# Windowed attention with a feed-forward layer on Trainium2: the order of the first loads, the split of the last stores, and a new table for the planner

## The chip, the core and the metric

The kernel runs on one core of one Trainium2 chip. A core has a matrix engine (TensorE, PE in the profile; its weight loads are PEld), VectorE (DVE), ScalarE (ACT), GpSimd (POOL) and SyncE (SP), each with its own instruction stream executed in order, and 16 DMA engines. SP and ACT issue the transfers here. The metric is the device time of one execution in microseconds.

## The reference

Eight batches of eight heads, 512 local and 32 global positions each, head size 64. Global queries attend to everything; local queries attend to the 32 global keys and to a window of 32 positions to either side. Then comes a feed-forward layer with a gate h - tanh(h).

```python
k_all = np.concatenate([k_g, k_l], axis=2)
v_all = np.concatenate([v_g, v_l], axis=2)
out_g = np.matmul(sm(scale * np.matmul(q_g, k_all.transpose(0, 1, 3, 2))), v_all)
s_ll = np.where(np.abs(pos[:, None] - pos[None, :]) <= 32, scale * np.matmul(q_l, k_l.transpose(0, 1, 3, 2)), -1e9)
s_lg = scale * np.matmul(q_l, k_g.transpose(0, 1, 3, 2))
out_l = np.matmul(sm(np.concatenate([s_lg, s_ll], axis=-1)), v_all)
x = np.concatenate([out_g, out_l], axis=2).transpose(0, 2, 1, 3).reshape(8 * 544, 512)
h = x @ w_in            # 512 -> 2048
return (h - np.tanh(h)) @ w_out
```

Here sm subtracts the row's maximum, takes the exponential and divides by the sum plus 1e-9.

## The kernel before

**Work and its parts.** The feed-forward layer runs in nine chunks: one of 512 local rows for each batch, and a last one, "g", with the 256 global rows of all batches. A chunk of local rows has 16 steps; each step has 12 matmuls into the hidden layer (L1136, or L1162 for the first steps of batch 0), then tanh on ACT (L1144), the subtraction on DVE (L1147), a rounding to the high part (L324, called through `copy`), the low part on POOL (L1153), and 12 matmuls into the output (L1199). Products that need precision are made of high and low parts in three passes.

The attention of the first two batches works on pairs of heads (class `Pair`): `add_load` brings keys and queries (L476), `add_turn` transposes them on PE (L493) and copies them into `first_kw` and `first_q`, `glob` copies the transposed global keys from `first_g` behind the windows of `first_kw`, `add_scores` makes the global queries' scores (L526, L527), their peaks on DVE (L532), exponentials on ACT (L537) and scaling on POOL (L545), turned on PE at L566; `add_local_scores` makes the local scores (L617), whose peaks are L884 (DVE), exponentials L891 (ACT), and scaling L904 (POOL), turned at L972. `add_products` multiplies with the values (L649). `add_first_globals` loads the global keys and queries of the first two batches (L435), one load for all eight heads, into `wraw3`. The later batches work head by head (class `Head`: L827, L828 for the global scores, L879, L880 for the local ones, L1053 and L1055 for products and turns), between the feed-forward matmuls of the batch before.

**Weights.** `add_weights` loads one of 32 tiles of 512 KB (L377), alternating between `wraw01` and a part of `first_q`; ACT rescales one half of each number (L388), DVE shifts the other (L392) and joins both (L397), the high part is rounded on ACT or DVE (L324), and POOL makes the low part (L403).

**Order.** Nothing is issued while it is written down: each step is given to `add` with its possible engines and costs, a due time, what it reads and writes, and its PSUM banks. `Order.run` then places the steps one by one: the one that can start earliest by the planner's own estimate, by due time among near equals, on the engine that suits. Due times and the penalties for one engine or the other come from the numbers in `CFG`. The dictionary `at` holds for each engine the time at which it is free, 0 at the start. What comes out is a fixed order for each engine.

**Transfers.** Nearly all are issued by SP. The first pair's keys and queries, four transfers, are issued by ACT; the global keys and queries and the first weights by SP. A chunk's output leaves through `out_copy` (a copy from PSUM to one of two buffers) and `out_dma`. For a local chunk the 128 rows of a tile lie together (L1229). For "g" a tile holds the 32 global rows of four batches, which lie 544 rows apart; L1231 writes them with one pattern of three dimensions:

```python
nc.sync.dma_start(bass.AP(out.tensor, out.offset + row * DM, [[step * DM, P // n], [DM, n], [1, DM]]), y)
```

Of the kernel before, what the change touches and what calls it, by code (L numbers as in the profile page):

```python
# [16 lines left out]
P = 128  # L17
# [32 lines left out]
class Order:  # L50
# [58 lines left out]
    def run(self):  # L109

        ready = [o for o in self.ops if o.n == 0]
        at = {}
# [5 lines left out]
        out = []  # L118
# [70 lines left out]
def kernel(ctx, tc, q_l, k_l, v_l, q_g, k_g, v_g, w_in, w_out, out):  # L189
    nc = tc.nc  # L190
# [3 lines left out]
    T = S + G  # L194
# [95 lines left out]
    def bank(shape, j, dt=F32):  # L290
# [6 lines left out]
        elif len(shape) == 4:  # L297
# [4 lines left out]
    CFG = dict(a_g=0.4467, a_gl=9.0702, a_kg=1.2994, a_kq=0.6435, a_ph=0.7195, a_qs=7.4639, a_v=2.7931, a_w=0.8782, a_wn=28.167, a_xg=24.0892,  # L302
               d_g=11.4807, d_gl=27.1005, d_kg=17.5448, d_kq=3.2824, d_ph=0.1724, d_pl=7.5682, d_qh=1.3047, d_qs=1.7431, d_tg=2.0404, d_tp=1.2696,
               d_v=43.1581, d_w=59.5639, d_wl=2.6144, d_wn=1.778, d_xg=14.9271, d_y=10.5287, gfirst=0, ho=12.4704, hs=5.8719, lag=14.1617, last=0.0,
               newb=2, o_ld=361.9221, o_pv=-2.1295, o_pvp=4.3749, o_s=-375.3617, o_sg=-28.1789, o_sp=31.7504, o_t=648.945, o_tg=45.2913,
               o_tn=-1106.6547, o_tpp=-433.7579, o_v=-410.0484, o_vr=-254.8525, one=0, p0=6.2738, pen=67.5481, penp=-32.1307, s_g=12.8404,
               s_gl=3.2481, s_kq=0.2136, s_p=46.7709, s_ql=1.9011, s_tg=1.375, s_v=8.7545, s_w=16.9623, s_wl=44.2573, step=15.8445, step1=4.7468,
               lag0=-307.9083, hs0=19.1353, tol=0.005, wd0=-185.6377, wsp=14.5594, xw=1.446, o_ld0=600.5133, o_tn0=224.9458, o_sg0=-83.4892,
               o_tg0=-104.0145, o_s0=-179.3281, o_sp0=-1012.5551, o_t0=617.9054, o_tpp0=232.7574, o_vl0=-205.8728, o_vl1=-1041.2318, o_pv0=816.5364,
               o_pvp0=61.9839, o_ld1=626.5193, o_pv1=-181.2357, o_pvp1=102.4522, o_s1=-119.6345, o_sg1=-827.2517, o_sp1=751.489, o_t1=311.7714,  # L310
               o_tg1=153.1303, o_tn1=-150.4646, o_tpp1=837.4523, o_v1=-236.5332, o_vr1=258.8109, wsp1=4.8097, ho0=596.7105, mw=0.0485, o_h0=507.8294,
               hp=-176.4382, bp0=180.6731, bp1=36.9715, bp2=87.4305, bp3=49.379, kd=0.0002)
# [115 lines left out]
    def add_first_globals(b):  # L428
# [4 lines left out]
        def load(a):  # L433
            def fn(e, _):
                nc.sync.dma_start(raw[a].rearrange("s (h d) -> s h d", h=H), (k_g, q_g)[a][b].rearrange("h s d -> s h d"))  # L435
            return fn
# [1020 lines left out]
```

## Time and profile before

| | |
|---|---|
| median of 3 runs (lowest to highest) | 1022.02 us (1020.94 to 1023.49) |
| the profiled execution's own time | 1022.42 us |
| its span, first to last instruction | 1020.6 us |
| PE busy | 991.1 us, 97% |
| DVE, ACT, POOL busy | 617.7, 653.3, 615.2 us |
| DMA moved | 91.67 MB, 90 GB/s on average |
| granted TensorE clock, mean | 0.997 |

The profile shows one execution. Busy times are of an engine's instructions alone; the times at which it waits, and who ended the wait, stand in a view of their own. Rows of the timeline give start and length in us, engine, line, operation, tiles written and read, how many were merged, and in brackets the idle time before and its releaser. "SPq" and "ACTq" are the sequencers that issue transfers: the length is that of the issue, not of the transfer.

### The profile page before, as it was taken

The numbers are of one execution on the slowest core, as the hardware profiler recorded it, in microseconds if no ns is written. First come the engines' busy times: TensorE is split into PE (matmuls) and PEld (weight loads), VectorE is DVE, ScalarE is ACT, GpSimd is POOL, SyncE is SP. The second block draws the span as 40 slices with busy tenths as digits, with TensorE's granted clock in tenths as the row PEclk, the third lists the DMA queues.
The fourth block names the chain that finished last, engine by engine and source line by source line (L and its number), as shares of the span: only waits on it lengthen the run. The fifth ranks groups of instructions, "written<-read, shape, count | busy, mean of one in ns | idle before, by whom it ended". The sixth has DMA issues, their size and how long they took to land.

```text
span 1020.6 us, 18634 instructions
## 1 busy us (share of the span) xinstructions
PE 991.1 (97%) x5648; PEld 825.3 (81%) x5648; DVE 617.7 (61%) x1877; ACT 653.3 (64%) x1732; POOL 615.2 (60%) x839
## 2 busy tenths in 40 slices
PE   6999999999999999999999999999999999999996
PEld 4777777887878888888888888888887888888895
DVE  6975665687758764777658774777657774221010
ACT  5867656776768765877568775887668774322221
POOL 4665656676767765677657775677657774322221
PEclk9999999999999999999999999999999999999998
DMA  8564644543354333543354432543255330100000
GB/s 212 142 161 142 175 125 101 131 88 81 70 124 103 83 84 68 132 89 83 64 116 110 89 84 57 143 88 84 57 109 122 83 74 10 42 1 1 31 11 22
DMA packets 250701, 91.67 MB, mean 90 GB/s; under 512 B 204520, under 2 KB 238056, under 8 KB 250600
## 3 DMA queue, kind: packets, MB, share of 16 engines
q1 hardware_dynamic: 248488, 89.95, 37.8%
q8 instruction: 45, 0.74, 0.3%
q10 hardware_dynamic: 2112, 0.52, 0.2%
q14 instruction: 56, 0.46, 0.1%
HBM read 49.27 MB, written 8.91 MB: 57 GB/s over the span
## 4 chain that ended last, share of the span: by engine, by line
PE 83%; ACT 5%; DVE 3%; issue 2%; DMA 2%; SPq 2%; POOL 2%; ACTq 0%; DVEq 0%; POOLq 0%
PE bank L1199 33%; PE bank L1136 30%; PE bank L1053 5%; PE bank L1055 4%; PE bank L879 2%; PE bank L880 2%; PE bank L649 1%; PE bank L972 1%; ACT prob L891 1%; PE bank L617 1%; PE bank L526 1%; PE bank L1162 1%; SPq L687 1%; DMA first_raw<-in_q_l_dram 1%; PE bank L493 1%
## 5 line engine op out<-in xcount | busy, mean ns | idle before, releaser
L1199 PE MATMUL bank<-w_out_hi,gates 128*128 128x512 f32 x1088 | 302.2, 396 | 0.7 <-ACT wraw L324 0.3
L1153 POOL TENSOR_TENSOR gates<-t,gates 128x512 fp32r<-128x512 f32 x136 | 175.4, 1290 | 177.9 <-PE bank L1199 128.0
L1199 PEld LDWEIGHTS bank<-w_out_hi,gates 128*128 128x128 f32 x1088 | 198.5, 188 | 42.9 <-POOL gates L1153 2.3
L1147 DVE TENSOR_TENSOR t<-bank,t 128x512 f32<-128x512 f32 x136 | 94.0, 692 | 170.8 <-ACT t L1144 169.5
L1144 ACT ACTIVATE t<-bank 128x512 f32<-128x512 f32 x136 | 81.3, 598 | 133.8 <-PE bank L1136 124.7
L1199 PE MATMUL bank<-w_out_lo,gates 128*128 128x512 f32 x544 | 152.3, 394 | 0.0
L1136 PE MATMUL bank<-x_hi,w_in_hi 128*128 128x512 f32 x496 | 137.5, 399 | 0.0
L1136 PE MATMUL bank<-x_hi,w_in_lo 128*128 128x512 f32 x496 | 133.7, 391 | 0.0
L1136 PE MATMUL bank<-x_lo,w_in_hi 128*128 128x512 f32 x496 | 133.5, 391 | 0.0
L904 POOL TENSOR_SCALAR prob<-prob,stats 128x224 f32<-128x224 f32 x240 | 107.8, 463 | 40.4 <-DVE stats L628 13.9
L324 ACT CAST gates<-t 128x512 fp32r<-128x512 f32 x136 | 84.3, 621 | 59.7 <-PE bank L1199 41.1
L891 ACT ACTIVATE prob<-prob,stats 128x224 f32<-128x224 f32 x240 | 113.7, 475 | 11.2 <-DVE stats L884 10.4
L1199 PEld LDWEIGHTS bank<-w_out_lo,gates 128*128 128x128 f32 x544 | 100.6, 188 | 20.1
L884 DVE CUSTOM_DVE_ANT_0 prob<-bank,mask 128x224 f32<-128x224 f32 x240 | 81.6, 388 | 51.6 <-PE bank L880 39.4
L1136 PEld LDWEIGHTS bank<-x_lo,w_in_hi 128*128 128x128 f32 x496 | 91.3, 188 | 18.4
L1136 PEld LDWEIGHTS bank<-x_hi,w_in_lo 128*128 128x128 f32 x496 | 90.9, 188 | 17.9
L324 ACT COPY wraw<-bank 64x288 f32<-64x288 f32 (+1 forms) x130 | 58.0, 446 | 69.2 <-PE bank L1053 45.3
L1136 PEld LDWEIGHTS bank<-x_hi,w_in_hi 128*128 128x128 f32 x496 | 87.8, 189 | 14.9 <-issue 0.4
L1055 PE MATMUL bank<-idr,prob 128*128 128x128 f32 x376 | 98.0, 280 | 0.4 <-DVE stats L839 0.2
L1053 PE MATMUL bank<-thi,vv 128*128 128x160 f32 (+2 forms) x384 | 96.8, 294 | 1.6 <-DVE stats L839 0.8
L1053 PE MATMUL bank<-tlo,vv 128*64 128x160 f32 (+2 forms) x384 | 89.3, 234 | 0.3 <-POOL tlo L951 0.3
L1088 POOL TENSOR_TENSOR x_lo<-wraw,x_hi 64x256 fp32r<-64x256 f32 x96 | 70.4, 734 | 29.3 <-DVE x_hi L324 20.9
(144 smaller groups left out, 1780.8 us busy)
## 6 DMA issues: line engine op xcount, KB each, us to landing
hl<-hl SPq DMA_DIRECT2D x72, 128.0 KB, 2.3
out_dram<-wraw SPq DMA_DIRECT2D x34, 256.0 KB, 2.4
kw<-hl SPq DMA_DIRECT2D x72, 96.0 KB, 2.2
wraw<-in_moe_w_in_dram SPq DMA_DIRECT2D x12, 512.0 KB, 4.7
rawkq<-in_k_l_dram SPq DMA_DIRECT2D x96, 64.0 KB, 2.3
rawkq<-in_q_l_dram SPq DMA_DIRECT2D x96, 64.0 KB, 2.3
vraw<-in_v_l_dram SPq DMA_DIRECT2D x48, 128.0 KB, 2.4
kw<-hl SPq DMA_DIRECT2D x72, 80.0 KB, 2.1
```

The source lines that it names most:

```text
L324: (nc.scalar.copy if e == "A" else nc.vector.tensor_copy)(dst, src)
L884: nc.vector.tensor_tensor_reduce(out=self.tile(t)[:, :KC], in0=getattr(self, f"s_{pair}")[:, i, :KC], in1=tile_mask[t], scale=-0.125, scal ...
L891: nc.scalar.activation(x, x, AF.Exp, bias=self.st[:, t:t + 1], scale=-1.0, accum_out=self.st[:, 4 + t:5 + t])
L904: nc.gpsimd.tensor_scalar(x, x, self.st[:, 8 + t:9 + t], 1.0, op0=ALU.mult, op1=ALU.mult)
L1053: nc.tensor.matmul(dst, l, r, start=i == 0, stop=i == len(mm) - 1, skip_group_check=True)
L1055: nc.tensor.transpose(*turns[i // each], idn)
L1088: eng[e].tensor_sub(places()[1], view(total, [(160, 2), (1, P)]), f32(places()[0]))
L1136: nc.tensor.matmul(self.h[s][:, j * n:(j + 1) * n], w[:, cc, f * P:(f + 1) * P], self.x()[xi][:, cc, :n], start=part == 0 and cc == 0 and ...
L1144: nc.scalar.activation(tt_[q], self.h[s], AF.Tanh)
L1147: nc.vector.tensor_sub(tt_[q], self.h.pop(s), tt_[q])
L1153: eng[e].tensor_sub(gg[q][1], tt_[q].rearrange("p (k c) -> p k c", k=4), f32(gg[q][0]))
L1199: nc.tensor.matmul(self.acc[tt], g[:, j * nt + tt], low_out(f) if wi else w_out_hi[:, f], start=s == 0 and k == 1, stop=last and k == 3 * ...
```

## The change

Four edits in the code, and a new table:

1. The first pair's keys stay on ACT's queue, its queries move to SP's queue; both come first, through due times of -1002 and -1001.
2. The global keys and queries of batch 0 move from SP to ACT, behind the first pair's keys (due time -1000).
3. For "g", each tile is written with four transfers of 32 rows in place of one: two from SP, two from ACT.
4. The planner takes every engine (T, A, D, P, S: PE, ACT, DVE, POOL, SP) to be free from 0.7 on, not from 0.
5. All numbers of `CFG` that set due times and penalties are new.

```diff
-        at = {}
+        at = dict.fromkeys("TADPS", 0.7)
...
-    CFG = dict(a_g=0.4467, a_gl=9.0702, a_kg=1.2994, a_kq=0.6435, a_ph=0.7195, a_qs=7.4639, a_v=2.7931, a_w=0.8782, a_wn=28.167, a_xg=24.0892,
+    CFG = dict(a_g=0.3833, a_gl=1.5118, a_kg=1.3108, a_kq=0.24, a_ph=0.0029, a_qs=9.8856, a_v=2.7859, a_w=0.9693, a_wn=28.6019, a_xg=24.9592,
...
-                nc.sync.dma_start(raw[a].rearrange("s (h d) -> s h d", h=H), (k_g, q_g)[a][b].rearrange("h s d -> s h d"))
+                eng[e].dma_start(raw[a].rearrange("s (h d) -> s h d", h=H), (k_g, q_g)[a][b].rearrange("h s d -> s h d"))
...
-            add(("S", 0.6), load(a), due - 100, w=[keys[a]], xfer=0.36)
+            add(("S" if b else "A", 0.6), load(a), due - 100 if b else -1000, w=[keys[a]], xfer=0.36)
...
-                add(("S" if self.j else "A", 1.1), load(a, (k_l, q_l)[a]), self.due(self.C["o_ld"] - 8) if self.j else -200 + a,
+                add(("S" if self.j or a else "A", 1.1), load(a, (k_l, q_l)[a]), self.due(self.C["o_ld"] - 8) if self.j else -1002 + a,
...
-                    def out_dma(e, _, tt=tt, key=key):
-                        y = wraw[key[1]]
-                        row, n, step = self.dst(tt)
-                        if n == P:
-                            nc.sync.dma_start(out[row:row + P, :], y)
-                        else:
-                            nc.sync.dma_start(bass.AP(out.tensor, out.offset + row * DM, [[step * DM, P // n], [DM, n], [1, DM]]), y)
+                    def out_dma(part):
+                        def fn(e, _, tt=tt, key=key):
+                            y = wraw[key[1]]
+                            for row, lo, hi in part:
+                                eng[e].dma_start(out[row:row + hi - lo, :], y[lo:hi])
+                        return fn
...
-                    add(("S", 0.6), out_dma, due + 0.5, r=[key], w=[("out", self.name, tt)], xfer=0.73)
+                    runs = self.dst(tt)
+                    k = max(1, len(runs) // 2)
+                    add(("S", 0.6 * k), out_dma(runs[:k]), due + 0.5, r=[key], w=[("out", self.name, tt)], xfer=0.73)
+                    if runs[k:]:
+                        add(("A", 0.6 * k), out_dma(runs[k:]), due + 0.5, r=[key], w=[("out", self.name, tt, 1)], xfer=0.73)
...
     def local_rows(b):
-        return lambda i: (b * T + G + i * P, P, 0)
+        return lambda i: [(b * T + G + i * P, 0, P)]
 
     def global_rows(i):
-        return i * (P // G) * T, G, T
+        return [((i * (P // G) + j) * T, j * G, (j + 1) * G) for j in range(P // G)]
```

What stands where now, at the places that the prediction speaks of. First SP's queue at the start of the program, with - for the rows of before and + for those of the changed kernel (`first_raw` and `rawkq` take keys and queries of a pair, `first_v` its values, `wraw_70` the global keys and queries, `wraw_65` and the weight load's `first_q` are the two buffers for raw weights):

```order
+L476 DMA first_raw<-in_q_l_dram 128x4x64 x2
+L588 DMA first_v<-in_v_l_dram 128x7x64
+L588 DMA first_v<-in_v_l_dram 96x64
+L588 DMA first_v<-in_v_l_dram 64x8x64
+L600 DMA first_v<-in_v_g_dram 32x4x64 x2
+L377 DMA wraw_65<-in_moe_w_in_dram 128x4x256
+L377 DMA first_q<-in_moe_w_in_dram 128x4x256
+L476 DMA first_raw<-in_k_l_dram 128x4x64 x2
+L476 DMA first_raw<-in_q_l_dram 128x4x64 x2
+L476 DMA rawkq<-in_k_l_dram 128x4x64 x2
+L476 DMA rawkq<-in_q_l_dram 128x4x64 x2
 L435 DMA wraw_70<-in_k_g_dram 32x8x64
```

Before, SP began with the two loads of L435 (batch 0's, now on ACT), then the two weight tiles, then the values; now it has the first pair's queries, then the values, then the two weight tiles. ACT at the same place, behind the program's first branch:

```order
 L476 DMA first_raw<-in_k_l_dram 128x4x64 x2
-L476 DMA first_raw<-in_q_l_dram 128x4x64 x2
+L435 DMA wraw_70<-in_k_g_dram 32x8x64
+L435 DMA wraw_70<-in_q_g_dram 32x8x64
 L324 ACT_TABLE_LOAD
-L324 COPY first_g<-bank_96 128x128
-L324 COPY first_m<-bank_96 64x4x32 x2
+L324 COPY first_g<-bank_97 128x128
+L324 COPY first_m<-bank_97 64x4x32 x2
 L388 ACTIVATE wraw_65<-wraw_65 128x512
 L324 COPY first_kw<-first_g 128x4x32 x2
```

The queries have left, the global loads have come; the broadcast of the global keys (`first_kw<-first_g`) stands behind the first weight step (L388) in both. DVE's first work on data, before:

```order
L324 COPY first_kw<-bank_95 128x2x160
L392 TENSOR_SCALAR wraw_65<-wraw_65 128x512
L397 SCALAR_TENSOR_TENSOR vraw<-wraw_65 128x512
L324 COPY first_q<-bank_97 128x512
L392 TENSOR_SCALAR first_q<-first_q 128x512
L532 ISA pg,stats<-bank_98,first_m 64x512
L532 ISA stats 64x1
L532 ISA pg,stats<-bank_99,first_m,stats 64x96
L532 ISA stats 64x1
L397 SCALAR_TENSOR_TENSOR wraw_66<-first_q 128x512
L884 ISA prob_92,stats<-bank_100,mask_89 128x224
```

and in the changed kernel:

```order
L324 COPY first_kw<-bank_95 128x2x160
L324 COPY first_q<-bank_96 128x512
L392 TENSOR_SCALAR wraw_65<-wraw_65 128x512
L397 SCALAR_TENSOR_TENSOR vraw<-wraw_65 128x512
L392 TENSOR_SCALAR first_q<-first_q 128x512
L397 SCALAR_TENSOR_TENSOR wraw_66<-first_q 128x512
L884 ISA prob_92,stats<-bank_98,mask_89 128x224
```

The copy of the queries comes ahead of the weights, both joins (L397) stand ahead of the first local peak (L884), and the global peaks (L532) have gone behind the local ones. Over the whole program 15 casts of `x_hi` from PSUM and 40 from `wraw` have moved from DVE to ACT, and two copies of `first_t` from ACT to DVE. Last, the end of ACT's order in the changed kernel, where the rows of 4x32x512 from SP were before:

```order
L1144 ACTIVATE t_67<-bank_96 128x512
L324 CAST gates<-t_67 128x4x128
L324 COPY wraw_65<-bank_101 128x512
L1229 DMA out_dram<-wraw_65 32x512 x2
L324 COPY wraw_65<-bank_99 128x512
L1229 DMA out_dram<-wraw_65 32x512 x2
```

Two transfers now stand between ACT's two copies, and two behind the second; SP has four of the same form. On PE, the order from the third batch on is nearly the one of before: in each batch there are two places where the score matmuls of a head's two halves stand next to each other, with the four hidden-layer matmuls that parted them moved behind.

More of the change, by code (lines that the diff above doesn't have):

```diff
@@ L299, in bank @@
         return t
-    CFG = dict(a_g=0.4467, a_gl=9.0702, a_kg=1.2994, a_kq=0.6435, a_ph=0.7195, a_qs=7.4639, a_v=2.7931, a_w=0.8782, a_wn=28.167, a_xg=24.0892,
[L303 to L312, printed above, removed]
@@ new lines @@
+    CFG = dict(a_g=0.3833, a_gl=1.5118, a_kg=1.3108, a_kq=0.24, a_ph=0.0029, a_qs=9.8856, a_v=2.7859, a_w=0.9693, a_wn=28.6019, a_xg=24.9592,
+               d_g=22.9208, d_gl=28.3456, d_kg=17.722, d_kq=0.8597, d_ph=6.695, d_pl=1.6149, d_qh=12.3091, d_qs=2.3107, d_tg=4.5597, d_tp=2.5431,
+               d_v=40.7113, d_w=58.5262, d_wl=5.2554, d_wn=0.1207, d_xg=17.1159, d_y=49.9741, gfirst=0, ho=11.9147, hs=5.7779, lag=10.5363, last=0.0,
+               newb=2, o_ld=275.9612, o_pv=-5.1163, o_pvp=5.2028, o_s=-239.3897, o_sg=-30.3435, o_sp=141.4394, o_t=780.0364, o_tg=173.9664,
+               o_tn=-1204.4747, o_tpp=-508.7815, o_v=-326.4365, o_vr=-559.4328, one=0, p0=22.6197, pen=88.2314, penp=-9.435, s_g=14.0824,
+               s_gl=5.4307, s_kq=9.1285, s_p=34.6177, s_ql=5.0621, s_tg=9.63, s_v=15.1668, s_w=18.0019, s_wl=29.0213, step=15.4752, step1=18.4221,
+               lag0=-447.7797, hs0=46.2469, tol=0.006, wd0=-88.6303, wsp=2.5132, xw=1.1559, o_ld0=617.7599, o_tn0=213.5168, o_sg0=-48.5134,
+               o_tg0=-174.1334, o_s0=-458.1335, o_sp0=-1034.3883, o_t0=493.7468, o_tpp0=135.0118, o_vl0=-307.4228, o_vl1=-1160.4087, o_pv0=987.1099,
+               o_pvp0=-28.2759, o_ld1=580.7539, o_pv1=-122.4085, o_pvp1=200.6386, o_s1=-352.0041, o_sg1=-755.7339, o_sp1=622.6201, o_t1=282.9062,
+               o_tg1=104.8414, o_tn1=269.9106, o_tpp1=736.3571, o_v1=-170.3736, o_vr1=35.2158, wsp1=17.3158, ho0=527.6724, mw=0.0018, o_h0=587.0606,
+               hp=-181.5994, bp0=212.1044, bp1=-104.67, bp2=174.2978, bp3=-230.6285, kd=0.0002)
```

## The prediction

> **What bounds the kernel now.** First the page: how much of the span TensorE (PE) is busy.
>
> ```profile
> span 1020.6 us, 18634 instructions
> PE 991.1 (97%) x5648; PEld 825.3 (81%) x5648; DVE 617.7 (61%) x1877; ACT 653.3 (64%) x1732; POOL 615.2 (60%) x839
> ```
>
> PE is idle for 29.5 us in all, and a change that alters no matmul can win little more. The windows view tells where that idle time lies (stretch, length, then busy time and count of PE, PEld, DVE, ACT and POOL, granted clock, DMA share, GB/s).
>
> ```profile
> 0.00:20.00 20.00, 10.06 (x55) 6.82 (x56) 11.19 (x50) 9.46 (x29) 8.34 (x24) 1.00 0.81 203
> 20.00:70.00 50.00, 48.02 (x386) 35.92 (x384) 44.99 (x167) 41.44 (x133) 31.66 (x49) 1.00 0.62 161
> 70.00:180.00 110.00, 109.01 (x605) 83.75 (x603) 66.59 (x175) 69.66 (x166) 66.17 (x69) 1.00 0.51 138
> 180.00:870.00 690.00, 682.25 (x3884) 577.78 (x3884) 473.58 (x1448) 495.48 (x1344) 473.91 (x671) 1.00 0.41 89
> 870.00:1011.00 141.00, 141.00 (x723) 120.80 (x722) 21.39 (x38) 36.65 (x61) 35.15 (x29) 1.00 0.04 16
> 1011.00:1021.00 10.00, 0.74 (x4) 0.28 (x2) 0.00 (x0) 0.59 (x2) 0.00 (x0) 0.68 0.17 52
> ```
>
> Idle PE time: 9.94 us in the first 20, 1.98 up to 70, 0.99 up to 180, 7.75 in the 690 us of steady work, none in the last chunk's matmuls, and then some 9 us at the very end, in which no engine does anything. So two places are worth something: the first 20 us and the last 9. Between 20 and 70 us VectorE (DVE) is busy 90% of the time; there it, too, can set the pace.
>
> Who ends PE's waits, from the waits view of PE (total, times, longest):
>
> ```profile
> PE bank L493 <- DMA first_raw<-in_k_l_dram: 4.9, 1, 4.9
> PE bank L493 <- DMA first_v<-in_v_g_dram: 3.9, 1, 3.9
> PE bank L566 <- POOL pg L545: 1.2, 1, 1.2
> ```
>
> The second one carries the wrong name: it ends at the transposes of pair 0's queries, which need the queries' second transfer. The timeline of the first 16 us shows the sequence (start, length):
>
> ```profile
> 0.74 1.02 ACTq L476 DMA_DIRECT2D first_raw<-in_k_l_dram  x2
> 1.67 0.46 SPq L377 DMA_DIRECT2D wraw<-in_moe_w_in_dram  x1
> 1.78 1.09 ACTq L476 DMA_DIRECT2D first_raw<-in_q_l_dram  x2
> 4.88 1.09 PE L493 MATMUL bank<-idr,first_raw 128*128 128x128 f32 x4 [4.88 <-DMA first_raw<-in_k_l_dram]
> 8.11 0.69 ACT L388 ACTIVATE wraw<-wraw 128x512 f32<-128x512 f32 x1 [0.79 <-DMA wraw<-in_moe_w_in_dram]
> 8.69 0.49 ACT L324 COPY first_kw<-first_g 128x128 f32<-128x128 f32 x2
> 10.46 1.09 PE L493 MATMUL bank<-idr,first_raw 128*128 128x128 f32 x4 [3.87 <-DMA first_v<-in_v_g_dram]
> 13.48 0.68 DVE L532 CUSTOM_DVE_ANT_0 pg<-bank,first_m 64x512 f32<-64x512 f32 x1 [0.68 <-PE bank L526]
> 13.70 2.14 PE L617 MATMUL bank<-first_kw,first_q 64*128 64x224 f32 x16
> 14.56 0.68 DVE L397 SCALAR_TENSOR_TENSOR wraw<-first_q 128x512 int32<-128x512 int32 x1
> 15.22 0.39 DVE L884 CUSTOM_DVE_ANT_0 prob<-bank,mask 128x224 f32<-128x224 f32 x1
> ```
>
> The keys are transposed at 4.88, the queries only at 10.46, the local scores (L617) run at 13.70, and the first local peak (L884) at 15.22.
>
> **The end: the one sure term.** The last two copies and transfers, what SP then waits for, the DMA share meanwhile, and for comparison the 32 row transfers of the local chunks (L1229: issue, and landing as min/median/max):
>
> ```profile
> 1010.42 0.59 ACT L324 COPY wraw<-bank 128x512 f32<-128x512 f32 x1 [4.36 <-PE bank L1199]
> 1011.03 1.93 SPq L1231 DMA_DIRECT2D out_dram<-wraw  x2
> 1011.77 0.59 ACT L324 COPY wraw<-bank 128x512 f32<-128x512 f32 x1 [0.77 <-PE bank L1199]
> ...
> SPq L1452 <- DMA out_dram<-wraw: 6.6, 1, 6.6
> ...
> 1014.00:1019.00 5.00, 0.00 (x0) 0.00 (x0) 0.00 (x0) 0.00 (x0) 0.00 (x0) 0.56 0.26 96
> ...
> L1229 SPq DMA_DIRECT2D out_dram<-wraw x32: 332/435/1048, 188.8 to 968.8; - x32
> DMA to landing us min/median/max: 2.0/2.4/3.6
> ...
> GB/s 0 0 0 0 0 0 0 0 0 0 0 0 47 386 386 398 328 386 386 410 269 0 0 0 0 0 0 0 246 398 410 398 269 410 386 410 71 0 0 0
> ```
>
> The last issue ends at 1011.03 + 1.93 = 1012.96, and 6.6 us later, at 1019.6, its data has landed; the span closes 1.0 us after that. While it runs, 0.26 of the 16 DMA engines, 4.2 of them, move 96 GB/s. The last row is the same 256 KB in the same 2 KB pieces at 965 to 970 us, written as one run of 128 rows: 390 to 410 GB/s, four times as much, landing after 2.0 us. The slow transfer is the one whose pattern has an outer dimension of 4. The changed kernel has no such pattern: four transfers of 32 rows for each tile, two from SP and two from ScalarE (ACT).
>
> New end, step by step: the first copy ends at 1011.01; ACT then issues two transfers, at 1.02 / 2 = 0.51 each as in the first row of the start, up to 1012.03; so the second copy begins 0.26 late, ends at 1012.62, and ACT's last issue begins at 1013.13. Landing 2.0 to 2.4 later: 1015.1 to 1015.5; I take 1015.2, 4.4 us earlier than 1019.6. Bounds: with the slowest landing of L1229, 3.6, it is 1016.7 (2.9 gained); with issues of 0.33 that do not delay the copy and a landing of 2.0, 1014.7 (4.9 gained).
>
> The Trainium skill, "DMA: Bandwidth & Descriptors", section "Why a DMA increments its semaphore by 16 and not by 1", says that a transfer is spread over the largest number of engines up to 16 that divides the slowest dimension on both sides: 4 for 4x32x512, 16 for 32x512. The trace agrees for the old shape (4.2 engines); no row shows the new one at its size. By this rule the term is the same. The same page's "Rules for kernel authors" speaks against the change: pieces of a tile's partitions share the same engines and should go as one transfer, and a second queue saves issue time alone; that is a rival below.
>
> **The start.** What the first 10 us moved, and what the SP queue waited for before its issues in the first 60 us; the last row is the page's median for a 512 KB weight load:
>
> ```profile
> q10 hardware_dynamic: 2112, 0.52, 23.4%
> wraw<-in_moe_w_in_dram SPq DMA_DIRECT2D x1, 512.0 KB, 6.4
> first_q<-in_moe_w_in_dram SPq DMA_DIRECT2D x1, 512.0 KB, 7.8
> first_raw<-in_q_l_dram ACTq DMA_DIRECT2D x2, 128.0 KB, 7.5
> ...
> SPq L476 <- DMA first_raw<-in_q_l_dram: 1.2, 1, 1.2
> SPq L600 <- DMA first_raw<-in_q_l_dram: 0.5, 1, 0.5
> ...
> wraw<-in_moe_w_in_dram SPq DMA_DIRECT2D x12, 512.0 KB, 4.7
> ```
>
> Queries: they take 7.5 us because two 512 KB weight loads of SP share the engines with them. ACT's queue (q10: keys and queries, 0.52 MB) needs 0.234 x 10 = 2.3 us of all 16 engines. With the queries first on SP's queue, keys and queries land together: not before 4.88, not after 4.88 + 2.3 = 7.2; I take 5.5. PE's wait of 3.9 us as it stands is gone.
>
> What is late next: the local scores also need the broadcast of the global keys (first_kw<-first_g), which in ACT's order stands behind L388, and that waits for the first weight tile. Before, this was ready at 8.69 + 0.49 = 9.2 and cost nothing. Now the first weights stand eighth on SP's queue, not third. The two SP waits above are on unrelated transfers eight places earlier in the program, so an issue waits for the landing of the eighth before it; for the first weight tile that is now the queries' second transfer. Issue at 5.5, landing 4.7 later, 10.2 (bounds: 4.88 + 4.7 = 9.6, 5.5 + 6.4 = 11.9). Add L388 and the broadcast, 0.69 + 0.49: L617 at 11.4 instead of 13.70, 2.3 us earlier (0.6 to 2.9).
>
> DVE comes after: in its new order the joins (L397) of both weight tiles stand ahead of the first peak. The second tile lands 7.8 - 6.4 = 1.4 later plus one issue of 0.46, at 12.1 (11.5 to 13.8); with L388 and L397, 0.69 + 0.68, the first peak is at 13.5 (12.9 to 15.2) instead of 15.22: 1.7 earlier. But before, DVE had by then also done the global peaks (L532, 14.56 - 13.48 = 1.08); these are still to do. Net 0.6 earlier (from 1.1 later to 1.2 earlier).
>
> **From 20 to 180 us** the pairs' steps stand in another order, and the casts of x_hi move from DVE to ACT. Of the 16 that DVE did, nine lie between 20 and 70 us; of the later form DVE did 40:
>
> ```profile
> L324 DVE CAST x_hi<-bank 128x256 fp32r<-128x256 f32 x9 | 3.7, 418 | 1.1 <-PE bank L649 1.1
> ...
> L324 DVE CAST x_hi<-wraw 64x256 fp32r<-64x256 f32 x40 | 22.1, 552 | 0.2
> ```
>
> DVE loses up to 3.7 of its 45.0 us, ACT rises from 41.4 to 45.1 of 50. The gain cannot exceed the 1.98 us that PE idles there; the loss, should ACT take over the pace, can reach the 3.7. I take 0.7 gained. Up to 180 us PE's idle 0.99 leaves nothing to win; the matmuls done before the first later head's scores are the same but for four.
>
> **From 180 to 1011 us** PE's order is the old one but for a spot in each batch where two pairs of score matmuls stand together instead of apart; the 40 casts moved to ACT (72% busy there) feed the next chunk, a batch later (six batches in 690 us, 115 us each). Zero, from 0.7 gained to 1.5 lost. 870 to 1011 has no idle time and stays.
>
> **Sum.** -4.4 - 0.6 - 0.7 = -5.7 us. The profiled execution took 1022.42 us, its span of 1020.6 and 1.8 around it, 0.40 above the median of the three runs; 1022.02 - 5.7 = 1016.3.
>
> **The rivals.**
> - *The whole of the start is won.* If the weights land by 9 us, DVE is not held, and the 3.9 us of PE's second wait go instead of 0.6: 1022.02 - 4.4 - 3.9 - 0.7 = 1013.0. For it: 4.7 is a median, so half of the weight loads land sooner. Against it: the issue of the first one waits for the queries.
> - *The weights are held longer.* SP's value issues stretch under backlog, the first weights land at 14 or later, and the start is 3 us worse instead of better: 1022.02 - 4.4 + 3 - 0.7 = 1019.9. For it: ACT and DVE each have a weight step ahead of the heads' work.
> - *The split gives nothing*: the 32-row transfers crowd on the same few engines, and only the 1.3 us of the other two terms remain: 1022.02 - 1.3 = 1020.7. Against it: 390 to 410 GB/s for the same 2 KB pieces where the outer dimension is 128. The rule of the Trainium skill on pieces of a tile, named above, leads here.
> - *Slower: the global heads' softmax becomes the wait.* The new order puts a pair's global scores behind its local ones, so POOL's scaling (L545) starts later; PE already waited 1.2 us once for it at L566. It decides as soon as L545 ends after the matmuls that PE has ahead of L566; if that comes back in all eight pairs, 8 x 1.2 = 9.6 are lost: 1022.02 - 4.4 + 9.6 = 1027.2. Against it: PE has matmuls of other pairs to put there.
>
> **Chances.** Forecast 0.55, whole start 0.25, weights held 0.09, split gives nothing 0.06, slower 0.05. About 0.3%, 3.1 us, is what a measurement of this kernel can tell from no change. Some of the forecast's own range reaches past 1018.9, so faster 0.81, same 0.14, slower 0.05. The range takes in the forecast with its bounds and the whole-start case down to 1011.5; upwards it reaches to 1020.0, into the held-weights case.
>
> **What would show it.** Right: the last landing about 2 us after the last issue at 390 GB/s or so, and the span closing near 1016 less what the start wins; the transposes of pair 0's queries at 5.5 to 7; L617 waiting for ACT's broadcast, and DVE's first L884 near 13.5. Wrong: a DMA share of 0.26 at the end; a wait of PE on L545 in every pair; DVE idle past 15 us on the weights; stalls in the steady 690 us beyond 9 us.

## The result, and the profile after

| | before | changed |
|---|---|---|
| median of six runs each | 1023.09 us (1020.94 to 1024.46) | 1014.47 us (1012.61 to 1015.90) |
| ratio | | 0.9916, 95% interval 0.9901 to 0.9932 |
| the profiled execution's own time | 1022.42 us | 1015.1 us |

The changed kernel is faster by 8.6 us (7.0 to 10.1). The two profiled executions differ by 7.3, within that interval; what follows accounts for the 7.3. The page of the changed kernel, busy time by engine:

```profile
span 1013.3 us, 18583 instructions
PE 991.5 (98%) x5648; PEld 826.4 (82%) x5648; DVE 605.8 (60%) x1826; ACT 669.2 (66%) x1783; POOL 613.5 (61%) x839
```

PE has the same work and 7.7 us less idle time: 1013.3 - 991.5 = 21.8 where it was 29.5. Where it went, by the windows view of the changed kernel:

```profile
0.00:20.00 20.00, 11.26 (x59) 8.13 (x60) 11.25 (x51) 9.65 (x29) 8.56 (x27) 1.00 0.89 221
20.00:70.00 50.00, 47.51 (x382) 35.25 (x381) 42.57 (x161) 43.29 (x140) 32.21 (x47) 1.00 0.58 159
180.00:870.00 690.00, 684.01 (x3884) 578.57 (x3883) 464.35 (x1407) 506.86 (x1380) 472.84 (x670) 1.00 0.41 89
870.00:1004.00 134.00, 134.00 (x692) 115.03 (x691) 20.20 (x35) 35.77 (x61) 32.64 (x28) 1.00 0.04 16
```

**The end.** The timeline of the changed kernel, from the last matmuls on, and SP's last wait:

```profile
1007.96 0.59 ACT L324 COPY wraw<-bank 128x512 f32<-128x512 f32 x1 [4.36 <-PE bank L1199]
1008.58 2.34 SPq L1229 DMA_DIRECT2D out_dram<-wraw  x4
1008.58 0.85 ACTq L1229 DMA_DIRECT2D out_dram<-wraw  x2
1008.90 0.39 PE L1199 MATMUL bank<-w_out_hi,gates 128*128 128x512 f32 x1
1009.53 0.59 ACT L324 COPY wraw<-bank 128x512 f32<-128x512 f32 x1 [0.98 <-PE bank L1199]
1010.15 0.85 ACTq L1229 DMA_DIRECT2D out_dram<-wraw  x2
...
SPq L1455 <- DMA out_dram<-wraw: 1.2, 1, 1.2
...
out_dram<-wraw SPq DMA_DIRECT2D x4, 64.0 KB, 1.7
out_dram<-wraw ACTq DMA_DIRECT2D x4, 64.0 KB, 1.9
...
1009.50:1012.30 2.80, 0.00 (x0) 0.00 (x0) 0.00 (x0) 0.59 (x1) 0.00 (x0) 0.91 0.65 182
```

SP's last wait is 1.2 instead of 6.6 us, and a transfer lands 1.7 to 1.9 after its issue. By the windows row, 0.65 of the 16 DMA engines move 182 GB/s from 1009.5 to 1012.3 us, where 0.26 moved 96 before. From the end of the last matmul, 1008.90 + 0.39 = 1009.29, to the end of the span it is 4.0 us. The same row of the kernel before gives 1020.6 - 1011.74 = 8.9:

```profile
1011.35 0.39 PE L1199 MATMUL bank<-w_out_hi,gates 128*128 128x512 f32 x1
```

So the end gives 4.9 of the 7.3 us, and the last matmul ends 2.4 earlier.

**The start.** The timeline of the changed kernel from the first transposes to the first peak, and SP's one wait for a transfer in its first 7 us:

```profile
4.86 1.94 PE L493 MATMUL bank<-idr,first_raw 128*128 128x128 f32 x8 [4.86 <-DMA first_raw<-in_k_l_dram]
4.59 1.08 SPq L600 DMA_DIRECT2D first_v<-in_v_g_dram  x2
5.72 0.43 SPq L377 DMA_DIRECT2D wraw<-in_moe_w_in_dram  x1
10.10 0.68 ACT L388 ACTIVATE wraw<-wraw 128x512 f32<-128x512 f32 x1 [1.95 <-DMA wraw<-in_moe_w_in_dram]
10.68 0.48 ACT L324 COPY first_kw<-first_g 128x128 f32<-128x128 f32 x2
11.21 3.36 PE L617 MATMUL bank<-first_kw,first_q 64*128 64x224 f32 x16 [3.79 <-ACT first_kw L324]
12.17 0.69 DVE L397 SCALAR_TENSOR_TENSOR wraw<-first_q 128x512 int32<-128x512 int32 x1 [0.29 <-ACT first_q L388]
13.22 0.39 DVE L884 CUSTOM_DVE_ANT_0 prob<-bank,mask 128x224 f32<-128x224 f32 x1 [0.36 <-PE bank L617]
...
SPq L588 <- DMA first_raw<-in_k_l_dram: 0.9, 1, 0.9
```

Keys and queries are transposed in one go of eight; then PE waits 3.79 us for the broadcast, which stands behind L388 and the first weights. L617 starts at 11.21 instead of 13.70, the first peak comes at 13.22 instead of 15.22. DVE's second join (L397) was done at 12.17 + 0.69 = 12.86; the 0.36 us from there to the peak DVE waited for PE's scores. The issue of the first weight load, at 5.72, follows directly on that of the last values (4.59 + 1.08 = 5.67).

**Up to the first later head.** Its first score matmul (L827) is a mark that both kernels pass. The windows view from the start to that mark, then the mark itself and the last L827 in the timeline, before:

```profile
0.00:176.85 176.85, 163.94 (x1028) 124.05 (x1029) 121.70 (x387) 118.92 (x321) 104.76 (x139) 1.00 0.57 152
...
176.85 0.41 PE L827 MATMUL bank<-kw,qgt 128*128 128x384 f32 x1 [0.99 <-DMA kw<-hl]
850.30 0.34 PE L827 MATMUL bank<-kw,qgt 128*128 128x384 f32 x1
```

and in the changed kernel:

```profile
0.00:174.52 174.52, 162.71 (x1025) 124.01 (x1025) 118.42 (x373) 121.63 (x333) 101.93 (x138) 1.00 0.57 154
...
174.52 0.41 PE L827 MATMUL bank<-kw,qgt 128*128 128x384 f32 x1 [0.58 <-DMA kw<-hl]
847.86 0.34 PE L827 MATMUL bank<-kw,qgt 128*128 128x384 f32 x1
```

The mark is passed 2.33 us earlier: 1.10 less idle time of PE (12.91 to 11.81) and 1.23 less busy time. From the first L827 to the last it takes 673.45 before and 673.34 after: the steady part gives nothing and takes nothing.

Single executions of one order differ here. Four profiled kernels have the order of before up to the mark (that kernel and three from the experiments on the end), and pass it at 176.47 to 176.89; four have the order of the changed kernel (that kernel, the one with the old store, and the two on the steady part), and pass it at 173.31 to 174.52. So the gain up to the mark is clear of the scatter, but a few tenths of a microsecond in one pair of profiles are not.

### The profile page after: what moved, and what is told of

Read it like the earlier page. It is cut to its first block, busy times and chain, and to the rows that moved or that the text cites. A ratio compares the mean times of both kernels' runs of the same rounds, so it can differ in the third digit from the quotient of the medians.

```text
span 1013.3 us, 18583 instructions
## 1 busy us (share of the span) xinstructions
PE 991.5 (98%) x5648; PEld 826.4 (82%) x5648; DVE 605.8 (60%) x1826; ACT 669.2 (66%) x1783; POOL 613.5 (61%) x839
## 4 chain that ended last, share of the span: by engine, by line
PE 84%; DVE 5%; ACT 2%; DMA 1%; issue 1%; SPq 1%; POOL 1%; ACTq 0%; DVEq 0%; POOLq 0%
PE bank L1199 34%; PE bank L1136 32%; PE bank L1053 5%; PE bank L1055 4%; PE bank L879 2%; PE bank L880 2%; DVE stats L898 1%; DVE prob L884 1%; DVE pg L839 1%; PE bank L827 1%; PE bank L649 1%; PE bank L972 1%; DVE tlo L989 1%; PE bank L617 1%; DMA wraw<-in_moe_w_in_dram 1%
## 5 line engine op out<-in xcount | busy, mean ns | idle before, releaser
L891 ACT ACTIVATE prob<-prob,stats 128x224 f32<-128x224 f32 x240 | 113.3, 474 | 10.2 <-DVE stats L884 8.2
L884 DVE CUSTOM_DVE_ANT_0 prob<-bank,mask 128x224 f32<-128x224 f32 x240 | 80.9, 388 | 55.4 <-PE bank L880 45.4
```

The costliest lines, as they stand in the source:

```text
L884: nc.vector.tensor_tensor_reduce(out=self.tile(t)[:, :KC], in0=getattr(self, f"s_{pair}")[:, i, :KC], in1=tile_mask[t], scale=-0.125, scal ...
L891: nc.scalar.activation(x, x, AF.Exp, bias=self.st[:, t:t + 1], scale=-1.0, accum_out=self.st[:, 4 + t:5 + t])
```

## The experiments

Each ratio is to runs of the kernel before on the same chip, with its 95% interval. Line numbers in the views are those of each kernel's own file, where an edit has moved the steps down by a few lines: L629 below is the changed kernel's L617, L896 its L884, L537 its L526.

### The end by itself

Four kernels. The kernel before, with the four row blocks of a tile as transfers of their own from two queues; the same from SP alone; each tile in two transfers with an outer dimension of 2, one from each queue; and the changed kernel with the old store.

```diff
# e1_tail_split_alone; e2_tail_split_sp_only has nc.sync four times
-nc.sync.dma_start(bass.AP(out.tensor, out.offset + row * DM, [[step * DM, P // n], [DM, n], [1, DM]]), y)
+for j, q in enumerate((nc.sync, nc.sync, nc.scalar, nc.scalar)):
+    r = row + j * step
+    q.dma_start(out[r:r + n, :], y[j * n:j * n + n])
# e3_tail_outer_two
+for j, q in enumerate((nc.sync, nc.scalar)):
+    q.dma_start(bass.AP(out.tensor, out.offset + (row + 2 * j * step) * DM, [[step * DM, 2], [DM, n], [1, DM]]),
+                y[2 * j * n:2 * j * n + 2 * n])
# e4_old_store_new_order: the changed kernel with the line that is removed above
```

> The kernel before, its order on every engine untouched; only the last chunk's two stores become four transfers of 32 rows each, two from SP and two from ACT. Theory (the pattern's outer dimension of 4 held the old store to about 4 of 16 DMA engines): from the end of the last matmul to the end of the span 4.0 us as in the changed kernel, not 8.9, DMA rate above 200 GB/s at the end, and 4.8 us less: about 1018.2 where the kernel before takes 1023.0. Rival (the stores ended early in the changed kernel for another reason, such as the queue being empty earlier): the end shrinks by less than 3 us.

> The kernel before with the same four transfers of 32 rows for each tile, all from SP. Theory (the shape matters, the second queue only saves issue time): four issues of some 0.35 to 0.4 us in a row, so the last one begins 0.5 to 0.8 us later than with two queues, and the time is 4.0 to 4.3 us below the kernel before. Rival (two queues are what made the stores fast): gain of 1 us or less, and a DMA rate near 100 GB/s at the end.

> The kernel before with two transfers for each tile, one from SP and one from ACT, each with a pattern of 2x32x512. Theory (the outer dimension sets the number of DMA engines, and the same ones for every transfer): two engines at 24 GB/s each, 48 GB/s for 512 KB, 10.7 us from about 1012, so the span ends near 1024 and the time is 3 to 4 us above the kernel before. If each queue had engines of its own, or the transfers took different ones, 96 GB/s and no change. Rival (smaller pieces on two queues are what helps): 3 us or more below the kernel before.

> The changed kernel with the old store (one pattern of 4x32x512 for each tile, from SP) and all else as changed, the order included. Theory (the two parts add up): 4.8 us above the changed kernel, that is about 1019.3, 3.7 below the kernel before, all of it won ahead of the last matmul. Rival (part of the gain of the order is only the earlier store): within 1.5 us of the kernel before.

| kernel | median us | ratio | last matmul to end of span, us |
|---|---|---|---|
| before | 1021.16 | | 8.9 |
| split, two queues | 1016.31 | 0.9954 (0.9942 to 0.9966) | 4.1 |
| split, SP alone | 1017.32 | 0.9965 (0.9953 to 0.9976) | 5.2 |
| outer dimension 2 | 1026.77 | 1.0056 (1.0044 to 1.0068) | 14.7 |
| changed, old store | 1018.30 | 0.9979 (0.9967 to 0.9992) | 8.9 |

The split alone is worth 4.7 us (3.5 to 5.9), the rest of the change 2.1 (0.8 to 3.4). That makes 6.8 where the whole change gave 8.6 (7.0 to 10.1), and by the ratios the split is worth 6.4 in the changed kernel (0.9979 - 0.9916 of 1021), more than the 4.8 expected; the intervals are too wide to show whether the two parts add up. Most of the split's worth is there with SP alone; the second queue adds 1.1 in the profile, which the intervals do not separate. Why it helps, in the kernel with an outer dimension of 2: the windows view of its tail (the last three numbers are the granted clock, DMA share and GB/s) and the packets from 1003 us on in the transfer view:

```profile
1013.00:1018.00 5.00, 0.00 (x0) 0.00 (x0) 0.00 (x0) 0.00 (x0) 0.00 (x0) 0.68 0.13 39
1018.00:1023.00 5.00, 0.00 (x0) 0.00 (x0) 0.00 (x0) 0.00 (x0) 0.00 (x0) 0.50 0.13 52
...
DMA packets 265, 0.53 MB, mean 23 GB/s; under 512 B 8, under 2 KB 8, under 8 KB 264
```

and the packets of the same stretch in the changed kernel:

```profile
DMA packets 384, 0.52 MB, mean 23 GB/s; under 512 B 128, under 2 KB 128, under 8 KB 384
```

With outer dimension 4 the share was 0.26 and the rate 96 GB/s; with 2 it is 0.13 and at most 52, which is 2.1 of 16 engines (0.13 x 16), and both queues together have no more. The small packets count the same way: 8 for four transfers of outer dimension 2, 128 for eight of 32 rows, that is 2 and 16 for each transfer; in the kernel before they are 8 for two transfers of outer dimension 4, that is 4 each. By the Trainium skill, "DMA: Bandwidth & Descriptors", section "Why a DMA increments its semaphore by 16 and not by 1", a transfer with a slowest dimension of 2 is spread over 2 engines: the trace agrees. The same page of the Trainium skill, in "Rules for kernel authors", advises against cutting a tile by its partitions because both halves spread over all 16 engines in any case. The uncut pattern here ran on 4.2 of them, so the reason does not apply, and the cut was worth 4.7 us.

### What holds the start

```diff
# e5_broadcast_first: the changed kernel, the broadcasts of the global keys ahead of the first L388 in ACT's order
+for j in range(2):
+    place[id(mark[f"glob{j}"])] = place[id(mark["rebias0"])] - 0.002 + 0.001 * j
# e6_weights_after_peaks: the same, and the steps on both first weight tiles (L388 to L403) behind the exponentials
+at = max(place[id(mark[f"exp{i}_{p}"])] for i in range(2) for p in range(2))
+for j in range(2):
+    for k, x in enumerate(("rebias", "low", "join", "high", "rest")):
+        place[id(mark[f"{x}{j}"])] = at + 0.001 * (1 + 5 * j + k)
# e13_second_tile_later: e5, and L388, L392 and L397 of the second tile alone behind the first pair's peaks
+x = max(place[id(mark[f"peak{i}_{p}"])] for i in range(2) for p in range(2))
+for k, n in enumerate(("rebias1", "low1", "join1", "load3", "high1", "rest1")):
+    place[id(mark[n])] = max(place[id(mark[n])], x + 0.001 * (1 + k))
# e7_values_behind_weights: the changed kernel, the first values behind the two weight loads on SP's queue
+place[id(mark["values0"])] = place[id(mark["load1"])] + 0.001
```

Here `place` is the planned time by which the steps are written down, and `mark` finds a step by its name; the lines that set these two up, and those that sort the steps again, are left out.

> The changed kernel with one step moved: on ACT the two broadcasts of the global keys for pairs 0 and 1 stand ahead of the first weight step (L388 in the changed kernel), so the local scores no longer wait for the first weight tile. Theory (DVE sets the pace there, since both weight joins stand ahead of the first peak): the local scores start at about 8.7 us and not 11.2, but the first peak stays near 13.2, and the end moves by less than 0.7 us. Rival (PE's wait of 3.8 us is on the path): what PE gains stays, and the time falls by 2 to 2.5 us, to about 1012.

> As the run with the broadcast first, and the steps of the first two weight tiles on ACT, DVE and POOL stand behind the first pair's exponentials. Theory (DVE's wait for the weights is what holds the start): the first peak at about 9.5 us, 3.7 earlier; but the weight steps, 2.2 us of DVE, come later, and the second pair's keys and queries land no earlier than 12 to 14 us, so 1 to 2 us below the changed kernel. Rival (pair 1's loads, or PE from 20 us on, set the pace): the end within 0.7 us of the changed kernel's.

> The changed kernel with one move on SP's queue: the first pair's values stand behind the first two weight tiles, whose issue then need not wait for the queries' landing. Theory (the values' place ahead of the weights is what shifted the wait): first weight tile in at about 7, local scores at about 8.5, first peak near 10 us, and 1 to 2.5 us less than the changed kernel, since DVE has done the weight steps by then. Rival (the queries then share the engines with 1 MB of weights again): queries land at 7 to 10 us as before the change, local scores at 11 or later, no gain or a loss of up to 2 us.

> The kernel of e5_broadcast_first, and the step on the second weight tile alone (L388 on ACT, L392 and L397 on DVE, and the load that reuses its buffer) goes behind the first pair's eight local peaks; PE's and SP's orders are those of e5. Theory, DVE is held by the second weight tile: the first peak comes at 11.0 to 11.3, right behind the first tile's join, instead of 12.36, the first later head's scores 0.5 to 1.3 earlier than 172.97, ratio to the kernel before 0.9895 to 0.990. Rival, DVE has the same work to do in either order and PE had other matmuls meanwhile: the first peak is earlier all the same, but the first later head stays at 172.5 to 174.5 and the ratio at 0.9905 to 0.9915.

| kernel | median us | ratio | L617 starts | first peak | first L827 |
|---|---|---|---|---|---|
| changed | 1014.47 | 0.9916 (0.9901 to 0.9932) | 11.21 | 13.22 | 174.52 |
| broadcast first | 1013.28 | 0.9908 (0.9893 to 0.9923) | 8.64 | 12.36 | 172.97 |
| and second tile later | 1012.38 | 0.9919 (0.9903 to 0.9935) | 8.37 | 10.61 | 172.20 |
| and both tiles after the exponentials | 1025.01 | 1.0030 (1.0018 to 1.0043) | 8.37 | 10.38 | 184.41 |
| values behind weights | 1015.15 | 0.9932 (0.9917 to 0.9946) | 11.98 | 14.00 | 175.57 |

In the kernel with both tiles moved, the next loads refill the two tiles' buffers before the steps read them, so the first two tiles of w_in hold other weights; instructions and sizes are the same.

The timeline of the kernel with the broadcast first and the second tile later:

```profile
8.02 0.50 ACT L332 COPY first_kw<-first_g 128x128 f32<-128x128 f32 x2
8.37 3.30 PE L629 MATMUL bank<-first_kw,first_q 64*128 64x224 f32 x16 [1.10 <-ACT first_kw L332]
10.00 0.69 DVE L405 SCALAR_TENSOR_TENSOR vraw<-wraw 128x512 int32<-128x512 int32 x1 [0.28 <-ACT wraw L396]
10.61 0.38 DVE L896 CUSTOM_DVE_ANT_0 prob<-bank,mask 128x224 f32<-128x224 f32 x1
15.73 1.07 PE L537 MATMUL bank<-first_kw,first_m 128*64 128x512 f32 x2 [1.42 <-DVE first_kw L332]
```

PE's wait for the broadcast falls from 3.79 to 1.10, and DVE's first peak comes 2.6 us before that of the changed kernel, as was meant. The first later head comes 2.3 earlier in this one execution, 1.1 ahead of the earliest of the four of the changed order, but the time of five runs does not follow: 0.9919 against 0.9916. With the broadcast first alone it is 0.9908, and the intervals overlap almost wholly. Part of the early start is given back at once: at 15.73 PE waits 1.42 us for DVE's copy of the next pair's keys, a wait that the changed kernel does not have there. No version here measurably beats the changed kernel. The quotient of the two medians for the last one, 1012.38 / 1022.33 = 0.9903, lies at the lower end of its interval, so a gain of one or two microseconds is not excluded; the 3.3 of the prediction's rival is.

With both tiles moved, 11.7 us are lost against the changed kernel (1.0030 against 0.9916). Its timeline and PE's longest wait:

```profile
20.44 0.67 ACT L397 ACTIVATE wraw<-wraw 128x512 f32<-128x512 f32 x1 [5.79 <-DMA wraw<-in_moe_w_in_dram]
...
PE bank L986 <- POOL t L917: 10.8, 1, 10.8
```

The first weight step runs at 20.44 instead of 10.10, since it waits for the load that overtook it, and ACT stands still for 5.79 us there. The edit made that wait itself, so this kernel does not tell how long the weights can be kept waiting; the kernel with the second tile alone was made because of it, with the load kept behind the step.

With the values behind the weights, the queries still land with the keys, but the global keys and queries, behind the first pair's keys in ACT's queue, come late:

```profile
5.32 1.94 PE L499 MATMUL bank<-idr,first_raw 128*128 128x128 f32 x8 [5.32 <-DMA first_raw<-in_k_l_dram]
9.48 0.66 PE L447 MATMUL bank<-idr,wraw 64*128 64x64 f32 x4 [2.22 <-DMA wraw<-in_q_g_dram]
```

They are transposed at 9.48, and the local scores start 0.8 us later than in the changed kernel. The ratio is higher by 0.0016, 1.6 us, within the intervals. Here it was the global loads that gave way to the weights, and not the queries.

### The code and the table, each without the other

One kernel has all edits of the code and the old `CFG`; the other has the code before with the new `CFG` and engines free from 0.7.

> The changed code (queries on SP's queue, global loads on ACT's, four tail transfers, engines free from 0.7) with the old table of due times. The planner then puts both weight tiles right behind the queries, and L388 and a cast ahead of the broadcast of the global keys. Theory, the start is made by the distance between queries and weights, and the loss in the steady part by the new table: queries share the engines with the weights as before, so L617 starts at 12 to 14, the first later head's scores at 176 to 177; between the ninth later head after that and the last one it takes 546 us as before; the tail after the last matmul is 4.1; ratio 0.9945 to 0.996. Rival, the new queues alone make the start, whatever the table: L617 at 8.5 to 11, first later head at 174.5 or less, and with the shorter steady part the ratio is 0.989 to 0.991.

> The kernel before with the new table and engines free from 0.7, nothing else: the first pair's queries stay behind its keys on ACT's queue, the global loads stay first on SP's, the last stores keep the pattern of 4x32x512. The planner puts the values ahead of the weights and the broadcast of the global keys ahead of L388. Theory, the table's order makes the start: queries no longer share the engines with the weights, L617 at 8 to 10, first later head at 173.5 to 175.5; the steady part takes 548 instead of 546; tail 8.9; ratio 0.997 to 0.999. Rival, the queries need a queue of their own: L617 at 12 or later, first later head at 176 or later, and with the longer steady part the ratio is 1.001 to 1.003.

| kernel | median us | ratio | first L827 | tail us |
|---|---|---|---|---|
| code, old table | 1019.71 | 0.9982 (0.9971 to 0.9994) | 177.04 | 4.1 |
| table, old code | 1023.61 | 1.0024 (1.0010 to 1.0039) | 178.57 | 8.9 |

Neither brings the 2.1 us of the rest of the change. The new code with the old table does at the start what its theory says, L617 at 12.84 and the first later head at 177.04, and has the short tail, yet it is 2.9 us worse than the split alone. PE idles 3.2 us between 20 and 70 us, where it was 2.0 before:

```profile
20.00:70.00 50.00, 46.76 (x372) 34.59 (x372) 44.07 (x166) 43.16 (x136) 32.55 (x47) 1.00 0.62 162
```

and from 177 us on it takes 2.5 longer, which stays unexplained. The new table with the old code is 4.6 worse than the changed kernel with the old store (1.0024 against 0.9979), from which it differs in the edits of the first loads and in what the planner makes of them. The ratio is the rival's, but not by the rival's reason, since its start is early:

```profile
6.85 1.09 PE L493 MATMUL bank<-idr,first_raw 128*128 128x128 f32 x4 [0.91 <-DMA first_raw<-in_q_l_dram]
10.09 2.48 PE L617 MATMUL bank<-first_kw,first_q 64*128 64x224 f32 x16
11.96 0.39 DVE L884 CUSTOM_DVE_ANT_0 prob<-bank,mask 128x224 f32<-128x224 f32 x1 [0.92 <-PE bank L617]
...
28.66 1.97 PE L526 MATMUL bank<-first_kw,first_m 128*64 128x512 f32 x2 [3.76 <-DVE first_kw L324]
...
20.00:40.00 20.00, 15.90 (x127) 11.54 (x126) 16.32 (x64) 15.68 (x51) 11.03 (x18) 0.91 0.55 151
```

The first peak is 1.3 us earlier than in the changed kernel, and the whole is slower: PE stops 3.76 us at 25 to 29 us for the copy of a later pair's keys, and the granted clock of that stretch is 0.91. Here an early start was given back within 20 us. The table and the queues are one change, not two. What the planner's 0.7 does by itself was not run; both kernels have it.

### The steady part

Between the tenth later head's first scores and the last head's, the changed kernel takes 2.7 us longer than the one before (548.72 against 545.98), although the whole from the first to the last is the same. Other executions of the two orders give 547.89 (the changed kernel with the old store) and 546.07 to 546.46 (the three kernels of the end with the order of before). Two things in its order could do it: the 40 casts of `x_hi` that moved from DVE to ACT, and the score matmuls of heads 2 and 6 of each batch, which now stand together.

```diff
# e8_casts_back_on_dve: the changed kernel, the 40 casts on DVE again, behind the step (L898) they stood behind before
...
+out = [(x, n, o, "D" if getattr(o.fn, "mark", None) in anchors else e) for x, n, o, e in out]
...
# e11_scores_parted: the changed kernel, four hidden-layer matmuls between the two halves again
...
+    if m[0][:3] == m[1][:3] == "scr" and m[0][:-2] in heads and m[0][:-2] == m[1][:-2] and m[2] == "hid":
+        place[id(pe[a + 1][2])] = pe[a + 2][0] + 0.0005
```

> The changed kernel with the 40 casts of x_hi from wraw done on DVE, the same ones as in the kernel before and behind the same step of the scores, where the change had moved them to ACT. In the profiles the changed kernel gives back some 0.45 us in each batch from 320 us on, 2.2 in five. Theory (the freed DVE runs into the wait behind POOL's long subtraction: L898 took 1.82 us instead of 0.63): the batches' intervals shrink by 0.4 us each, about 2 us less at the end. Rival (the loss comes from the score matmuls that now stand together): the intervals stay, the end moves by less than 0.7 us.

> The changed kernel, but the score matmuls of heads 2 and 6 of each batch from the fourth on are parted again by the four hidden-layer matmuls that stood between the two halves before; nothing else moves. Theory, the score matmuls that stand together cost the steady part its 2.5 us (the second half's peak comes late on DVE): from the tenth later head to the last one 546 us instead of 548.5, ratio 0.989 to 0.990. Rival, the loss comes from the order on the other engines: still 548 to 549, ratio 0.9915 as for the changed kernel.

| kernel | median us | ratio | tenth to last later head, us |
|---|---|---|---|
| casts on DVE again | 1014.49 | 0.9923 (0.9910 to 0.9936) | 548.54 |
| scores parted | 1014.60 | 0.9932 (0.9918 to 0.9946) | 550.30 |
| code, old table | 1019.71 | 0.9982 (0.9971 to 0.9994) | 546.89 |
| table, old code | 1023.61 | 1.0024 (1.0010 to 1.0039) | 549.01 |

Both theories fell: neither edit brings the stretch back to 546. It goes with the new table (549.0 with the old code, 546.9 the other way round), and the same table makes the stretch ahead of it shorter: from the first to the tenth later head 124.62 us in the changed kernel, 127.47 before. Which step of the order shifts the time from the one to the other stays open. It has no part in the result, since the two cancel.

## Why the prediction was right, step by step

**The end: right in mechanism, 0.5 too small.** Forecast 4.4 us with bounds of 2.9 and 4.9; the profile shows 4.9, the split alone 4.7. ACT's issues took 0.85 / 2 = 0.43 instead of 0.51, the second copy was held up by 0.98 - 0.77 = 0.21 instead of 0.26, and transfers landed after 1.7 to 1.9 instead of 2.0 to 2.4. The rate that was named as a sign, 390 GB/s or so, did not come: 182 on average, with the second tile's transfers beginning 1.6 us after the first's (1010.15 and 1008.58). The rival in which the split gives nothing is refuted by the split alone, whose interval ends at 0.9966.

**The start: the times near, two of them for another reason.** L388 came at 10.10 (forecast 10.2), L617 at 11.21 (11.4), the first peak at 13.22 (13.5), and the releaser of L617 was the broadcast, as written. The weight load was forecast to be issued at 5.5, when the queries have landed; it was issued at 5.72, and no wait for the queries stands ahead of it. It followed on the values, whose issue had itself waited 0.9 us for the first pair's keys. The first peak was forecast from DVE's joins. These were done at 12.86, and the peak waited 0.36 us longer for PE, whose scores took 3.36 us where the forecast took the 2.14 of before for granted (last section). That the two paths ended so close together is luck.

PE's idle time of the first 20 us fell by 1.20 where 0.6 was forecast, at the upper bound of 1.2. But what the forecast reckoned by, that the first peak's time and DVE's order set the gain, did not hold: in the experiments the peak came 2.6 us earlier at no gain that can be told. The rival "the whole of the start is won" came nearer in size, 9.0 us of gain against 8.6 measured, where the forecast had 5.7. Its mechanism did not come about: the first weights landed at 10.1, not by 9, PE still waited 3.79 us, and in the kernel in which DVE was not held by the second tile the 3.3 us that it priced did not appear.

**20 to 180 us: the step that failed.** "I take 0.7 gained" was argued from DVE's relief. The relief came, 44.99 to 42.57 us of DVE, with ACT up from 41.44 to 43.29. Yet PE's idle time from 20 to 70 us rose from 1.98 to 2.49. The other executions bear it out: it is 1.32 to 1.98 us in the four with the order of before, 2.14 to 2.52 in the four with the new one. So less work on DVE did not shorten PE's waits there. What PE waited for in the changed kernel is, above all, one copy on ACT and one on DVE:

```profile
PE bank L493 <- ACT first_t L324: 1.0, 1, 1.0
PE bank L493 <- DVE first_kw L324: 0.7, 1, 0.7
```

Whether moving either of the two would win time was not run. From 70 us to the first later head idle time fell by 0.41 (0.99 to 0.58), where nothing was forecast, but over the four executions of each order this stretch does not differ clearly (0.31 to 0.99, and 0.23 to 0.66). Together with the start that makes 1.20 - 0.51 + 0.41 = 1.10 of idle time, near the 1.3 forecast for both, by errors that cancel. The other 1.23 are busy time of PE up to the mark. The forecast named a difference of four matmuls there and gave it no price; the trace has three fewer, about 3 x 163.94 / 1028 = 0.5, and 0.7 are left that the profile does not break down further. In the four executions of the old order it is 163.94 to 165.08 us, in those of the new 162.71 to 162.93, so the ranges do not meet.

**The steady part: right.** Forecast zero, measured 0.11 from first to last L827. That it is made of 2.9 won and 2.7 lost was not seen.

**The slower rival** rested on POOL's scaling. PE has no wait at L545's result in the changed kernel; the 1.2 us at L566 are gone.

In sum, forecast 4.4 + 0.6 + 0.7 = 5.7; the profiles show 4.9 + 1.1 + 1.2 + 0.1 = 7.3 and the runs 8.6 (7.0 to 10.1). The time lies in the range, the sign and the order of the terms held, and the sum was too small, by half a microsecond at the end and by the busy time in the first 175 us.

## What to carry to other kernels

Look at the DMA share of a last, uncovered transfer. Here 0.26 meant that a pattern with an outer dimension of 4 ran on about four of 16 engines, and cutting it there was worth more than a second queue (3.6 us with SP alone, 4.7 with both queues). A stage whose engine is 90% busy is not thereby the pace: with 2.4 us less work on DVE, PE idled 0.5 us longer. Look at which single wait of the bounding engine ends last, and try moving it before pricing it. A planner's table is made for one set of queues; tested without the other, each half of such a change can lose, as both did here against the kernel with the same last store and neither half (2.9 and 2.4 us).

## What the hardware showed beyond this

The first local scores ran slower in the changed kernel although they are the same 16 matmuls. The groups view by shape (busy us, mean ns), before at 13.0 to 14.5 us, before at 14.5 to 15.7, and changed:

```profile
L617 PE MATMUL bank<-first_kw,first_q 64*128 64x224 f32 x4 | 1.0, 602 | 0.0
...
L617 PE MATMUL bank<-first_kw,first_q 64*128 64x224 f32 x14 | 1.6, 366 | 0.0
...
L617 PE MATMUL bank<-first_kw,first_q 64*128 64x224 f32 x16 | 3.4, 594 | 3.8 <-ACT first_kw L324 3.8
```

Before, PE had been at work without a gap since 10.46, and its matmuls became fast at about 14.5, 4 us later. In the changed kernel PE began again at 11.21, and all 16 ran at the slow speed, 1.2 us longer; so of the 2.5 us by which L617 came earlier, half were left at its end (14.57 against 15.84). It was not the long stand-still of 3.8 us that made them slow: in the kernel with the broadcast first and the second tile later PE stood still for 1.10 us alone, and the same 16 took 3.30. PE had not been fast yet in either. The granted clock of the profile reads 1.00 in the first 20 us of both kernels, so this row does not show it; the durations do.

What a stand-still does to a PE that is already fast is seen in the kernel with the new table and the old code:

```profile
16.66 1.07 PE L526 MATMUL bank<-first_kw,first_m 128*64 128x512 f32 x2 [2.23 <-DVE stats L541]
28.66 1.97 PE L526 MATMUL bank<-first_kw,first_m 128*64 128x512 f32 x2 [3.76 <-DVE first_kw L324]
...
29.00:34.00 5.00, 5.00 (x34) 3.35 (x34) 4.63 (x12) 2.37 (x5) 1.57 (x2) 0.70 0.06 11
```

After 2.23 us of idle time the two matmuls took 1.07 us, after 3.76 they took 1.97, and here the granted clock shows it, 0.70 from 29 to 34 us. The Trainium skill, "TensorE: Matmul & The Clock Gate", Part 1 on the HAM clock gate, describes it: half speed until about 4 us of sustained work, and again after an idle stretch of some 3.4. The durations here agree with the first by the 4 us before, and with the second by the stops of 2.23 and 3.76 us; the slow matmuls took 594 to 602 ns against 366, which is less than double. Work that is brought forward to a PE that is not yet fast starts at the slow speed, and a forecast of its duration should not take the row of a PE that was already running.
